# A fused attention and two-MoE kernel: batch 1 goes through the first MoE in two groups of tokens

## The chip, the cores and the metric

The kernel runs on one core of a Trainium2 chip. The metric is device time in microseconds of one execution, lower is better.

## The reference, cut to what matters

Four batches of 576 tokens, 8 heads of 64. Each row of scores keeps its 32 largest values; the attention output goes, token by token, through a dense "first MoE" (two products with 1536 columns, multiplied, and a product back to 512) and then through a second MoE in which each token goes to the one of 8 experts that its gate picks.

```python
scores = scale * np.matmul(q, k.transpose(0, 1, 3, 2))        # (4, 8, 576, 576)
kth = np.partition(scores, -top_k, axis=-1)[..., -top_k:-top_k + 1]
attn = softmax(np.where(scores >= kth, scores, -1e9))
x = (attn @ v) laid out as (2304, 512)
x = ((x @ w_a) * (x @ w_b)) @ w_out                            # first MoE, d_ff 1536
expert_idx = np.argmax(x @ w_gate, axis=1)                     # second MoE
out[mask] = gate_w[mask, None] * (np.maximum(x[mask] @ w1[e], 0) @ w2[e])
```

## The kernel before, in words

**Work and order.** The kernel is written as a list of operations with an engine, an estimated cost, a position and dependencies (class `Plan`). `Plan.emit` runs a list schedule over them once, when the program is built: at each step an engine takes the ready operation of the lowest position. What comes out is a fixed order for each engine; on the chip each engine runs its own list in that order and waits wherever an input is missing. SyncE issues the loads and stores, also in one fixed order.

**Attention.** The 576 tokens of a batch are two groups: g0 has 320 tokens, g1 has 256 (`GRP`). A head pair (p = 0 to 3) with a group is worked in tiles of 128 query rows: 5 tiles for g0, 4 for g1. A tile is: scores on TensorE (L601), copied by ScalarE (L606), the 32nd largest found on VectorE by MAX8 and MATCH_REPLACE8 (L625 to L652), the exponential on ScalarE (L633), masked on VectorE (L680), transposed on TensorE (L706). After the tiles of a group the product with v follows, which is called the *av* here: L727 and, last, L731. There are 8 av in a batch, 32 in all. Positions of attention are 10 times the tile's number, so attention goes ahead of everything else that is ready.

**Units.** Keys and queries of a head pair are loaded and prepared once for a *unit* (`load_unit`, `prep_unit`): k, q and v are loaded, k and q are split in a high and a low part (`hl`: ScalarE L512, GpSimd L514), transposed on TensorE (L523, 18 of 128x128), copied by ScalarE (L528, L531 and four small ones), and the transposed keys are copied once more by two DMAs (kS, L542). The buffers of raw k, raw q and `hl` exist once. The first 8 units (`FU`) take a shorter way in which k and q stay whole.

**First MoE.** `moe1(b, groups, xf, pos)` is called for the groups of a unit set when their attention is done. Its positions lie 1e5 higher than those of attention, so its matmuls fill what attention leaves of TensorE. It goes over 12 blocks of d_ff in two halves of 6. `ab` (L824) takes one weight block `wt` of 1 MiB (L802) and, for each group in `groups`, 24 matmuls; `l2` (L854) takes one block of 0.75 MiB (L842) and, for each group, 18 matmuls. A pass therefore loads 12 + 8 weight blocks, whatever the number of groups in it. `wt` has 3 buffers. A batch needs 288 L824 and 144 L854 matmuls with 320 columns (g0), and as many with 256 columns (g1). Then `gating(b, x2, groups, fill)` picks experts and scatters the rows.

**What sets the groups.** Batch 0 is in `HALVES`: its units are four for g0 and then four for g1, and `moe1` is called twice. The batches 1 to 3 have units that hold both groups, and `moe1` is called once, after the batch's last av:

```python
    for b in range(B):
        sets = [(g,) for g in (0, 1)] if b in HALVES else [(0, 1)]
        for groups in sets:
            for p in range(HP):
                for g in groups:
                    ...
                units.append((b, p, len(tiles), groups))
...
            if p == HP - 1 and g == groups[-1]:
                moe1(b, groups, XF[b], pos + 3)
```

After batch 3's attention the experts of the second MoE follow (L1136 to L1301), on rows that all batches have scattered. In the first 300 us the weights of the first MoE are also converted and stored (`conv`), and 8 fills of the scatter target are written (L345).

Of the kernel before, what the change touches and what calls it, by code (L numbers as in the profile page):

```python
# [209 lines left out]
def fused_kernel(ctx: ExitStack, tc: tile.TileContext, q, k, v, w_a, w_b, w_out, w_gate, w1, w2, out,  # L210
                 opts=None, dbg=None):
    nc = tc.nc
    opts = opts or {}
# [14 lines left out]
    OOB = 1.0e6  # L228
    HB = FB // 2
    CW = 512  # L230
    HALVES = opts.get("halves", (0,))
    FU = opts.get("fu", range(8))
    PE, ACT, DVE, POOL, SP = "PE", "ACT", "DVE", "POOL", "SP"

# [1074 lines left out]
# [3 lines that stand above are left out]
# [274 lines left out]
```

## Time and profile before

| | |
|---|---|
| median of 3 runs (range) | 1232.25 us (1228.04 to 1233.31) |
| the profiled execution's own time | 1233.15 us |
| its span in the trace | 1231.4 us |
| mean granted TensorE clock | 0.956 of 2.4 GHz |
| TensorE busy | 1103.6 us, 90% |
| VectorE busy | 896.3 us, 73% |
| ScalarE, GpSimd busy | 718.1 us, 460.6 us |
| DMA | 215.49 MB, mean 175 GB/s |

PE is TensorE, PEld its weight loads, DVE VectorE, ACT ScalarE, POOL GpSimd, SP SyncE. A row of busy time by stretch gives the stretch (us from the span's start), its length, then for PE, PEld, DVE, ACT and POOL (those that take part) busy us and the number of instructions, then the granted clock, the busy share of the DMA engines, and GB/s. A row of the timeline gives start, duration, engine, line, operation, tile written <- tiles read, shapes and count; in brackets the idle time just before, and what ended it. A row of costs gives the count, busy us and mean ns of one, then the idle time before. A row of DMA issues ends with KB of each and the median us from issue to landing; "q" behind an engine is its queue. L12 is line 12 of the kernel.

### The profile page before, as it was taken

Reading aid. Unit: us, or ns where it says so; the run is one execution under the profiler, and the core shown is the slowest. Engines: PE = TensorE matmul, PEld = TensorE weight load, DVE = VectorE, ACT = ScalarE, POOL = GpSimd, SP = SyncE. Lnnn points to the kernel's source line nnn. Section 1 sums busy time; section 2 is a strip of 40 time slices with the busy share of each in tenths; the row PEclk is TensorE's granted clock in tenths of the full one; section 3 lists DMA queues with packets and bytes.
Section 4 is the critical chain, followed back from the end, with each engine's and each line's share of the span. In section 5 each row is a group of like instructions: output and inputs, shape, how many; then the busy total and the mean of one; then the engine's idle time right before and its main releaser. Section 6 shows DMA issues by size and latency. Waiting matters only on the chain.

```text
span 1231.4 us, 22514 instructions
## 1 busy us (share of the span) xinstructions
PE 1103.6 (90%) x7710; PEld 981.2 (80%) x7710; DVE 896.3 (73%) x2636; ACT 718.1 (58%) x1567; POOL 460.6 (37%) x622
## 2 busy tenths in 40 slices
PE   4656796979999789999999999999999999999996
PEld 2333474868888579889888998989999899999996
DVE  6999999999998999999998999910004545444441
ACT  6667676776667567666765766633224445544551
POOL 3455566755536234234535422455234100000001
PEclk9966798989999999999999999999899999999998
DMA  8487578999677234244243442246535655554450
GB/s 235 130 276 229 164 245 261 323 303 300 208 255 248 93 87 144 109 153 144 78 152 112 132 151 104 86 155 225 191 147 184 189 152 174 176 177 151 159 177 22
DMA packets 116863, 215.49 MB, mean 175 GB/s; under 512 B 28883, under 2 KB 77011, under 8 KB 109061
## 3 DMA queue, kind: packets, MB, share of 16 engines
q1 hardware_dynamic: 113525, 204.52, 52.4%
q0 software_dynamic: 3216, 9.46, 2.0%
q8 instruction: 63, 1.03, 0.4%
q14 instruction: 59, 0.48, 0.1%
HBM read 171.82 MB, written 35.25 MB: 168 GB/s over the span
## 4 chain that ended last, share of the span: by engine, by line
PE 55%; DVE 14%; DMA 11%; issue 8%; ACT 7%; POOL 4%; SPq 1%; POOLq 0%; ACTq 0%; DVEq 0%
PE ab L824 16%; PE ab L854 9%; PE ab L1182 5%; PE pv L727 5%; DVE am L680 3%; DVE m L638 3%; PE ms L1231 3%; PE pv L1231 3%; PE sp L601 3%; DVE kt L641 2%; PE tp L706 2%; DMA xsort<-rows,pi 2%; DMA rawk<-in_k_dram 2%; DMA wt<-wos 1%; PE pv L731 1%
## 5 line engine op out<-in xcount | busy, mean ns | idle before, releaser
L824 PE MATMUL ab<-xh,wt 128*128 128x320 f32 (+1 forms) x1344 | 303.9, 304 | 3.9 <-ACT sb L809 3.8
L824 PEld LDWEIGHTS ab<-xh,wt 128*128 128x128 f32 x1344 | 227.6, 191 | 13.2 <-issue 7.8
L824 PE MATMUL ab<-xl,wt 128*128 128x320 f32 (+1 forms) x672 | 199.9, 297 | 0.0
L638 DVE MATCH_REPLACE8 m<-kt,m 128x288 f32<-128x288 f32 x432 | 188.5, 440 | 0.0
L641 DVE MAX8 kt<-m 128x8 f32<-128x288 f32 x432 | 182.3, 444 | 0.5
L854 PE MATMUL ab<-gH,wt 128*128 128x320 f32 (+1 forms) x768 | 171.8, 305 | 4.5 <-DMA wt<-wos 4.5
L680 DVE SCALAR_TENSOR_TENSOR am<-s,kt,e 128x576 f32<-128x576 f32 x144 | 139.8, 996 | 0.3
L854 PEld LDWEIGHTS ab<-gH,wt 128*128 128x128 f32 x768 | 130.7, 193 | 6.7 <-DMA wt<-wos 3.9
L832 POOL TENSOR_TENSOR sa<-sa,sb 128x320 f32<-128x320 f32 (+1 forms) x96 | 79.6, 829 | 145.0 <-ACT sb L809 144.5
L824 PEld LDWEIGHTS ab<-xl,wt 128*128 128x128 f32 x672 | 128.8, 192 | 0.0
L633 ACT ACTIVATE e<-s,nm 128x576 f32<-128x576 f32 x144 | 108.6, 778 | 11.6 <-POOL nm L628 11.3
L854 PE MATMUL ab<-gT,wt 128*128 128x320 f32 (+1 forms) x384 | 115.1, 300 | 0.0
L1256 POOL DMA_INDIRECT out_dram<-y,ti x23 | 23.0, 999 | 227.6 <-ACT y L1250 212.6
L1100 DVE TENSOR_TENSOR wp<-raw,wp 128x1024 fp32r<-128x1024 f32 (+1 forms) x73 | 67.4, 942 | 55.6 <-ACT wp L1099 55.2
L606 ACT COPY s<-sp 128x576 f32<-128x576 f32 x128 | 81.9, 640 | 42.9 <-PE sp L601 23.7
L706 PE MATMUL tp<-idr,am 128*128 128x128 f32 x512 | 84.8, 304 | 20.3 <-ACT aT L710 7.2
L401 POOL TENSOR_TENSOR gT<-sa,gH 128x320 fp32r<-128x320 f32 (+1 forms) x96 | 84.6, 881 | 45.8 <-ACT gH L400 45.4
L706 PEld LDWEIGHTS tp<-idr,am 128*128 128x128 f32 x512 | 64.1, 155 | 38.6 <-ACT aT L710 15.8
L1182 PE MATMUL ab<-xgh,wp 128*128 128x304 f32 (+6 forms) x352 | 89.4, 312 | 1.1 <-DVE gT L1189 0.7
L710 ACT COPY aT<-tp 128x512 f32<-128x512 f32 x128 | 72.4, 587 | 26.6 <-PE tp L706 25.8
L727 PE MATMUL pv<-aT,vt 128*64 128x320 f32 (+1 forms) x512 | 79.2, 451 | 6.5 <-ACT aT L695 4.5
L809 ACT ACTIVATE sa<-ab 128x320 f32<-128x320 f32 (+1 forms) x120 | 49.4, 412 | 53.9 <-PE ab L824 30.7
(303 smaller groups left out, 2560.8 us busy)
## 6 DMA issues: line engine op xcount, KB each, us to landing
wt<-ws SPq DMA_DIRECT2D x54, 1024.0 KB, 5.6
wt<-wos SPq DMA_DIRECT2D x44, 768.0 KB, 5.7
raw<-in_moe_w_dram SPq DMA_DIRECT2D x64, 512.0 KB, 3.7
kS<-kT SPq DMA_DIRECT2D x24, 304.0 KB, 4.5
xsort<-rows SPq DMA_DIRECT2D x8, 771.0 KB, 14.4
wp<-ws SPq DMA_DIRECT2D x6, 1024.0 KB
vt<-in_v_dram SPq DMA_DIRECT2D x20, 256.0 KB, 3.1
gT<-in_moe_w_a_dram SPq DMA_DIRECT2D x8, 512.0 KB, 4.1
```

The lines of the kernel that those rows point to most:

```text
L401: P(POOL, c_pool(cost), pos, lambda: nc.gpsimd.tensor_sub(lo(), src(), fr(hi())), r=rd + wh, w=wl)
L606: P(ACT, c_act(S), pos, lambda hf=hf, sp=sp: nc.scalar.copy(s()[:, :, hf * HS:(hf + 1) * HS], sp()[:, :, 0:HS]), r=[sp], w=[(s, (h, hf)) f ...
L633: P(ACT, c_act(S, True) + 90, pos, lambda h=h, e=e: nc.scalar.activation(e(), s()[:, h], AF.Exp, bias=nm()[:, h], scale=SCALE), r=[(s, (h, ...
L638: P(DVE, c_dve(HS), pos + 5.0 * h, lambda x=x, h=h, j=j: nc.vector.match_replace(out=m()[:, h], in_to_replace=kt(j, 8 * x - 8, 8 * x), in_ ...
L641: P(DVE, c_dve(HS), pos + 5.0 * h, lambda x=x, h=h, j=j: nc.vector.max(out=kt(j, 8 * x, 8 * x + 8), in_=m()[:, h]), r=[(m, h)], w=[KT(j, x)])
L680: P(DVE, c_dve(S) + 60, pos, lambda: nc.vector.scalar_tensor_tensor(am(), sc(), kth(), e(), op0=OP.is_ge, op1=OP.mult, accum_out=r.sum()[: ...
L706: res = nc.tensor.transpose(tp()[:, 512 * h + x * 128:512 * h + (x + 1) * 128], z()[:, 640 * h + x * 128:640 * h + (x + 1) * 128], idf)
L727: nc.tensor.matmul(pv()[64 * h:64 * h + 64, 0:n], u.vt()[:, h, j, :], r.aT[h]()[:, j, 0:n], start=(j == 0), stop=False)
L824: res = nc.tensor.matmul(pa()[:, 0:n], view()[:, m, wi, ko, :], xv()[:, ko], start=(ko == 0 and x == 0), stop=(ko == KO - 1 and x == 2))
L832: P(POOL, c_pool(n), pos, lambda: nc.gpsimd.tensor_mul(sa()[:, 0:n], sa()[:, 0:n], sb()[:, 0:n]), r=[sb], w=[sa])
L854: res = nc.tensor.matmul(pa()[:, 0:n], wv()[:, wi, f, :], gv()[:, f, :], start=(f == 0 and x == 0), stop=(f == HB - 1 and x == 2))
L1182: res = nc.tensor.matmul(pa()[:, 0:cap], p1[ko]()[:, wi, f * 128:(f + 1) * 128], xv()[:, ko], start=(ko == 0 and i == 0), stop=(ko == KO - ...
```

## The change

Batch 1 joins batch 0 in `HALVES`.

```diff
@@ -228,7 +228,7 @@
     OOB = 1.0e6
     HB = FB // 2
     CW = 512
-    HALVES = opts.get("halves", (0,))
+    HALVES = opts.get("halves", (0, 1))
     FU = opts.get("fu", range(8))
```

Batch 1 then has 8 units in place of 4: g0 of the four head pairs, then g1 of them. Its tiles are the same 36 in another order. `moe1` and `gating` are called for g0 after batch 1's fourth av and for g1 after its eighth. `FU` stays at 8 units, so batch 1's units all go the long way of `prep_unit`.

Since the schedule is made anew, the fixed orders shift from the 9th av on. The first place is TensorE just before the 16th av, which ends batch 1's attention; `tp` and `pv` are PSUM tiles, `am` the masked exponentials, `xh` and `xl` the parts of the first MoE's input, `hl` the split keys or queries. Before:

```order
L706 MATMUL tp<-idr,am 128x128 x8
L715 MATMUL pv<-idr,am 128x128
L601 MATMUL sp<-kT,qT 128x288
L601 MATMUL sp<-kS,qT 128x288
L601 MATMUL sp<-kT,qT 128x288
L601 MATMUL sp<-kS,qT 128x288
L523 MATMUL tp<-idr,hl 128x128 x4
L727 MATMUL pv<-aT_4907,vt 64x256
```

The same place now:

```order
L706 MATMUL tp<-idr,am 128x128 x4
L715 MATMUL pv<-idr,am 128x128
L824 MATMUL ab<-xh_2929,wt 128x320
L824 MATMUL ab<-xl_2942,wt 128x320
L824 MATMUL ab<-xh_2929,wt 128x320 x2
L824 MATMUL ab<-xl_2942,wt 128x320
L824 MATMUL ab<-xh_2929,wt 128x320
L523 MATMUL tp<-idr,hl 128x128 x4
L727 MATMUL pv<-aT_5312,vt 64x256
```

Matmuls of batch 1's g0 now stand between its last attention tiles. Between the 8th and the 16th av 660 matmuls of L824 and L854 stood before; now there are 762.

The second place is SyncE after the last fill of the scatter target, where units of batch 1 are loaded. `wt` are weight blocks of the first MoE, `rawk`, `rawq`, `vt`, `kS` belong to a unit. Before:

```order
L542 DMA kS<-kT 64x1216 x2
L842 DMA wt<-wos 128x1536
L802 DMA wt<-ws 128x2048
L440 DMA rawk<-in_k_dram 128x2x256
L440 DMA rawk<-in_k_dram 64x64
L802 DMA wt<-ws 128x2048
L440 DMA rawk<-in_k_dram 64x64
L440 DMA rawq<-in_q_dram 128x2x256
L440 DMA rawq<-in_q_dram 64x64 x2
L802 DMA wt<-ws 128x2048 x4
L842 DMA wt<-wos 128x1536
L440 DMA vt<-in_v_dram 128x2x256
```

The same place now:

```order
L542 DMA kS<-kT 64x1216 x2
L802 DMA wt<-ws 128x2048
L440 DMA rawk<-in_k_dram 128x2x256
L802 DMA wt<-ws 128x2048
L440 DMA rawk<-in_k_dram 64x64 x2
L440 DMA rawq<-in_q_dram 128x2x256
L440 DMA rawq<-in_q_dram 64x64 x2
L802 DMA wt<-ws 128x2048 x3
L842 DMA wt<-wos 128x1536
L440 DMA vt<-in_v_dram 128x2x256
```

Between a unit's keys (kS) and the next unit's first load (vt) eight weight blocks stood before, and six stand there now, since a unit of batch 1 is now one group long. Over the program there are 66 loads of L802 into `wt` in place of 54, 52 of L842 in place of 44, and four more units' loads.

The third place is TensorE at the 32nd and last av; `gH` and `gT` are the parts of the first MoE's inner result, all of batch 2 here. Before:

```order
L731 MATMUL pv<-aTt,vt 64x256 x2
L854 MATMUL ab<-gH_8125,wt 128x256
L854 MATMUL ab<-gT_8138,wt 128x256
L854 MATMUL ab<-gH_8125,wt 128x256 x2
L854 MATMUL ab<-gT_8138,wt 128x256
L854 MATMUL ab<-gH_8125,wt 128x256 x2
L854 MATMUL ab<-gT_8138,wt 128x256
L854 MATMUL ab<-gH_8125,wt 128x256 x2
```

The same place now:

```order
L731 MATMUL pv<-aTt,vt 64x256 x2
L854 MATMUL ab<-gH_8318,wt 128x256
L854 MATMUL ab<-gT_8330,wt 128x256
L854 MATMUL ab<-gH_8318,wt 128x256 x2
L854 MATMUL ab<-gT_8330,wt 128x256
L854 MATMUL ab<-gH_8318,wt 128x256
L854 MATMUL ab<-gH_8088,wt 128x320
L854 MATMUL ab<-gT_8113,wt 128x320
```

Before, 126 matmuls of batch 2 (54 with 320 columns, 72 with 256) stand between the last av and the first gating matmul of batch 2; now 42 do (18 and 24). From that gating matmul on TensorE's order is the same to the end.

## Rows read from the trace of the kernel before

**Rows 1.** The page: busy time, share of the span and instructions of each engine.
```profile
PE 1103.6 (90%) x7710; PEld 981.2 (80%) x7710; DVE 896.3 (73%) x2636; ACT 718.1 (58%) x1567; POOL 460.6 (37%) x622
```
**Rows 2.** Busy time by stretch, all engines, from batch 1's start to the end.
```profile
235.00:335.00 100.00, 89.21 (x649) 79.15 (x647) 95.40 (x307) 69.93 (x159) 54.98 (x71) 0.97 0.87 278
335.00:395.00 60.00, 57.01 (x465) 51.78 (x462) 57.41 (x186) 42.82 (x104) 28.75 (x41) 1.00 0.71 235
395.00:460.00 65.00, 53.21 (x365) 44.02 (x366) 60.57 (x196) 40.13 (x91) 20.61 (x34) 0.92 0.34 111
460.00:807.00 347.00, 339.30 (x2595) 308.70 (x2593) 320.03 (x1029) 228.83 (x529) 138.57 (x203) 1.00 0.38 124
807.00:1232.00 425.00, 404.94 (x2826) 389.40 (x2824) 143.69 (x292) 173.80 (x350) 85.97 (x116) 0.98 0.50 163
```
**Rows 3.** Busy time by stretch of lines L824 and L854 alone, after the last av.
```profile
807.80:1232.00 424.20, 83.92 (x576) 79.95 (x576) 0.98 0.50 163
...
807.80:1232.00 424.20, 58.30 (x414) 56.75 (x414) 0.98 0.50 163
```
**Rows 4.** Timeline of TensorE: the last av, and the pace of matmuls behind it.
```profile
807.14 0.65 PE L731 MATMUL pv<-aTt,vt 64*64 64x256 f32 x4
...
808.06 0.40 PE L854 MATMUL ab<-gH,wt 128*128 128x256 f32 x2
...
808.42 0.40 PE L854 MATMUL ab<-gH,wt 128*128 128x256 f32 x2
...
811.37 0.46 PE L854 MATMUL ab<-gH,wt 128*128 128x320 f32 x2
...
811.81 0.46 PE L854 MATMUL ab<-gH,wt 128*128 128x320 f32 x2
```
**Rows 5.** Busy time by stretch, in steps of 10 us, late in batch 1.
```profile
416.00:426.00 10.00, 6.12 (x41) 5.64 (x41) 10.00 (x32) 4.47 (x9) 3.59 (x7) 0.97 0.14 54
426.00:436.00 10.00, 8.81 (x50) 6.12 (x48) 10.00 (x37) 6.44 (x15) 2.00 (x5) 0.68 0.12 29
```
**Rows 6.** A unit's preparation: timeline of TensorE, then costs on ACT and POOL.
```profile
224.72 0.54 PE L523 MATMUL tp<-idr,hl 128*128 128x128 f32 x5
225.10 0.38 PE L854 MATMUL ab<-gH,wt 128*128 128x320 f32 x1
...
L512 ACT CAST hl<-rawk 128x576 fp32r<-128x576 f32 x12 | 8.1, 676 | 4.5 <-DMA rawk<-in_k_dram 4.5
...
L531 ACT CAST kT<-tp 128x512 fp32r<-128x512 f32 x24 | 14.1, 589 | 2.7 <-PE tp L523 2.4
...
L514 POOL TENSOR_TENSOR hl<-rawk,hl 128x576 fp32r<-128x576 f32 x12 | 17.8, 1483 | 14.3 <-ACT hl L512 14.2
```
**Rows 7.** Costs of gating on VectorE: the longest and shortest of its 12 operations.
```profile
L967 DVE TENSOR_TENSOR gb<-gb 128x24 f32<-128x24 f32 (+2 forms) x6 | 1.9, 312 | 0.1
...
L1005 DVE TENSOR_TENSOR cntb<-ms,cntb 128x8 f32<-128x8 f32 x6 | 1.0, 160 | 0.1
```
**Rows 8.** Chain of waits and timelines: a late weight block in batch 0's g1 pass.
```profile
388.61 6.26 DMA wt<-wos
...
395.01 0.36 PE L854 MATMUL ab<-gH,wt 128*128 128x256 f32 x1 [1.38 <-DMA wt<-wos]
...
401.47 0.76 DVE L614 TENSOR_TENSOR m<-sp,s 128x576 f32<-128x576 f32 x1 [3.39 <-ACT s L606]
```
**Rows 9.** DMA issues in 235 to 335 and 335 to 460; then 10 us by stretch.
```profile
wt<-ws SPq DMA_DIRECT2D x9, 1024.0 KB, 9.6
...
wt<-ws SPq DMA_DIRECT2D x10, 1024.0 KB, 5.6
...
286.00:296.00 10.00, 10.00 (x81) 8.71 (x80) 10.00 (x30) 7.20 (x17) 6.17 (x8) 1.00 1.05 318
```
**Rows 10.** Chain of waits: preparation of the unit after batch 1's end.
```profile
438.68 2.97 DMA rawk<-in_k_dram
...
442.53 1.75 POOL hl L514
```

## Prediction

> **What bounds the kernel now.** I read the page's engine table first, then busy time by stretch, then TensorE's timeline where a stretch looked odd, and last the chain of waits. TensorE is busy 90% of the span, VectorE 73% [rows 1], but these are averages over stages with different limits [rows 2]. From 235 to 460 us, batch 1's attention, VectorE is busy 95 to 96% and sets the pace; TensorE has holes: 10.8 us in the first 100, 3.0 in the next 60, and 11.8 in the last 65. In those last 65 us batch 0's first MoE has run out and batch 1's may not start, because its one call waits for the batch's last av; the clock falls with it, 0.92 on the mean, 0.68 in the worst 10 us [rows 5]. From 460 to 807 us TensorE is busy 98% and VectorE 92%: both are near their limit, and matmuls pile up. After the last av, which ends at 807.8 us [rows 4], VectorE has little to do and TensorE sets the end, 424 us long.
>
> What lies behind the last av is the point. 576 L824 and 414 L854 matmuls run there [rows 3]. Batch 3 by itself has 576 and 288, so 126 L854 matmuls are batch 2's, left over: a debt that goes back to the hole at 395 to 460.
>
> **The change part by part.**
>
> *Term 1, behind the last av: minus 11.1 us.* The new order leaves 42 matmuls of batch 2 there, 84 fewer: 36 with 320 columns, 48 with 256. Their pace there is three in 0.44 us (811.37 to 811.81) and three in 0.36 us (808.06 to 808.42) [rows 4], so 0.147 and 0.120 us each, and 36 x 0.147 + 48 x 0.120 = 5.3 + 5.8 = 11.1 us. All of it lies on the path, since TensorE does nothing else there and its order behind is the same. The cover shrinks from 16.6 us of matmuls to 5.5 (18 x 0.147 + 24 x 0.120); batch 3's g0 matmuls, whose input is ready by then, cover what comes after, so I cost the shorter cover at nothing. If they did not, the price would be a few tenths of a microsecond.
>
> *Term 2, TensorE up to the last av: plus 0.2 us.* Added: the same 84 matmuls, 11.1 us; four more unit preparations of 18 transposes, five of which take 0.38 us (224.72 to 225.10) [rows 6], so 72 x 0.076 = 5.5 us; a second set of gating matmuls, some 0.6 us by the same pace. That is 17.2 us. Recovered: between the 8th and the 16th av 762 matmuls stand where 660 stood, among the tiles where nothing stood before. If the stretch from 395 to 460 becomes like its neighbour behind, its 11.8 us of idle time go, and 8% of 65 us of slow clock, 5.2 us [rows 2]: 17.0 us. Both ends: if the 3.0 us before it go too, minus 2.8; if nothing could be filled, plus 17.2.
>
> *Term 3, VectorE up to the last av: nothing on the path, at most 2.3 us.* The second gating adds 12 operations of 160 to 312 ns, 2.3 us in sum [rows 7]. They fall after 433 us, where VectorE has 27 us of idle time [rows 2]. Without that cover they cost 2.3.
>
> *Term 4, ScalarE and GpSimd: nothing.* A unit's preparation costs ScalarE two splits of 0.68, four copies of 0.59 and about 1 us of small ones, 4.7 us, and GpSimd two of 1.48 [rows 6]: 18.9 and 11.9 us for four units, among 225 us in which they are idle about 72 and 121 us [rows 2]. If the cover fails, a unit starts late: see the third rival.
>
> *Term 5, weight blocks: plus 3.4 us.* Batch 1 loads 20 blocks more, 12 of 1 MiB and 8 of 0.75, 18 MiB; four units add 1.4 MiB each by their shapes (k, q and v of 288 KiB, two copies kS of 304 KiB). On average there is room, as the DMA engines are busy 71%, 34% and 38% from 335 us on [rows 2]. But a block in a pass of one group feeds 18 matmuls of 0.120 us, 2.2 us, or 24, at most 3.5 us, while a block takes 5.6 us to land, and 9.6 us when the DMA engines are crowded [rows 9]; with three buffers it arrives in time only if attention stands in between. The trace has one case where it did not, in batch 0's g1 pass: a block landed 6.26 us after its issue, TensorE waited 1.38 us, and VectorE, waiting for scores behind that, 3.39 us [rows 8]. Batch 0's two passes loaded 40 blocks; batch 1's two passes load as many, so I take one more such wait. Ends: 0 if every block is early, and for the other end the fourth rival.
>
> *Term 6, the crowded start: nothing taken, at most 7 us.* By the 11th av the new order wants three blocks and one unit more than before, 4.4 MiB; at the 318 GB/s of the most crowded 10 us [rows 9] that is 14.5 us of transfer, in a stretch of 100 us whose DMA share is 0.87 [rows 2]. The 13 us of room would nearly do. If they do not, I price it at half the transfer, 7 us. The Trainium skill, "Perfetto Trace Analysis", section "Identifying the Most-Contended Engine", says to judge DMA by bytes against the memory's peak, not by the engines' occupancy; by its 358 GB/s the 278 GB/s here leave 22% free and the bound would be 0. The rows speak against the page: landing went from 5.6 to 9.6 us at that rate.
>
> *Sum.* 1233.15 us (the profiled execution, 0.9 above the median shown) - 11.1 + 0.2 + 3.4 = 1225.7, so **about 1225 us** against the median of 1232.25, or 0.6% faster. A measurement of this kernel can tell about 0.5%, 6.2 us, from no change: faster means below 1226.1, slower above 1238.4.
>
> **The rivals.**
>
> *Second case, attention ends earlier.* From 460 to 807 us TensorE may be the slower of the two: only 7.7 us idle. Between the 16th and the last av the new order has 786 - 720 = 66 fewer matmuls with 320 columns and 48 more with 256, 9.7 - 5.8 = 3.9 us less, and the rest of the hole (3 us) goes. If TensorE alone paces there, the last av comes 7 us earlier: 1225.7 - 7 = 1219, or 1215 without the weight wait. [...]
>
> *Third case, units come late: no difference.* A unit of batch 1 is now 4 or 5 tiles long in place of 9, and raw k, raw q and the split exist once. At the next boundary after batch 1 the chain of waits does run through it: 2.97 us for raw k, 1.75 us for the split [rows 10], though VectorE was not idle. Four more boundaries of 2 us each, 8 us, or the 7 us of term 6, would give 1232 to 1234.
>
> *Fourth case, slower: weight blocks decide.* If the passes of batch 1 meet late blocks not once but six times (15% of 40 blocks), each costs VectorE 3.4 us as at 395 us, and batch 2's attention starts 20 us later: 1233.15 - 10.9 + 20.4 = 1243. The point is (6.2 + 10.9) / 3.4, five waits. For it: 3.5 us of work against a landing of 5.6. Against it: batch 0's 40 blocks, in a far more crowded stretch, met one.
>
> That the change does not do what it says is excluded by the new order.
>
> **How the numbers follow.** My forecast, with its own range of 1219 to 1229, has 0.45; the second case 0.14; the third, with term 6, 0.27; the fourth 0.14. The forecast lies at the edge of the 0.5%: I put 0.38 of its 0.45 below 1226.1. So faster is 0.38 + 0.14 = 0.52. The remaining 0.07 and the 0.27 of the third case make 0.34 within 0.5%. Slower is 0.14. The range for 8 in 10 reaches from 1214, the second case with 1 us to spare, to 1240, which takes in the third case and the beginning of the fourth.
>
> **What would show it.** Right: 576 and 330 matmuls of L824 and L854 behind the last av; that av within 5 us of 807; in batch 1's last 65 us TensorE busy over 95% at full clock. Term 5 is wrong if waits for `wt` in front of L824 or L854 are none, or several. The forecast falls if the last av comes more than 9 us later than 807: then the hole was filled and VectorE paid for it. The third case shows as idle time in front of L523 or L601 at each boundary of batch 1's units; the fourth as TensorE idle in front of L824 and L854, ended by a DMA into `wt`.

## The result: slower by 0.8%, and the profile after

| | before | after |
|---|---|---|
| median of 7 runs each, measured together | 1232.32 us | 1243.12 us (1241.43 to 1247.2) |
| ratio, 95% interval | | 1.0082 (1.006 to 1.0105) |
| profiled execution, its span | 1233.15, 1231.4 us | 1242.58, 1240.9 us |
| 16th av (end of batch 1's attention) | 433.1 us | 460.9 us |
| from the 16th to the 32nd av | 374.3 us | 374.2 us |
| from the 32nd av to the end | 424.0 us | 405.8 us |

The last three rows are the starts of an av's last L731 matmul, counted in the trace; they add up to the span. Such a column comes from one profile of each kernel; runs 4, 15 and 16 below, which leave batch 1 as it was, have their 16th av at 428.3 to 439.9 us, so a difference there of less than some 12 us decides nothing by itself. The forecast was 1225 us, so it was wrong by 18 us and by its sign. The loss has one place: 27.8 us more up to the 16th av. Behind the last av 18.2 us are won, more than was forecast.

The page's engine line answers to [rows 1]: every engine is busy a little longer.

```profile
PE 1111.5 (90%) x7790; PEld 987.8 (80%) x7790; DVE 900.4 (73%) x2648; ACT 733.9 (59%) x1608; POOL 475.8 (38%) x629
```

Seen from TensorE, the 9.5 us that the span grew are 7.9 us more of busy time and 1.6 more of idle time (span less busy: 127.8 us before, 129.4 now). The idle time that the change was to take away is all still there.

Busy time by stretch, cut at the same times as [rows 2]:

```profile
235.00:335.00 100.00, 79.03 (x546) 69.55 (x543) 78.84 (x237) 63.12 (x146) 49.22 (x55) 0.88 0.87 269
335.00:395.00 60.00, 56.30 (x448) 50.35 (x446) 49.74 (x165) 39.99 (x100) 28.42 (x46) 0.97 0.74 248
395.00:460.00 65.00, 62.83 (x500) 57.25 (x500) 61.88 (x199) 50.33 (x118) 39.13 (x50) 1.00 0.77 249
460.00:807.00 347.00, 334.23 (x2555) 302.74 (x2552) 327.22 (x1066) 230.40 (x529) 133.75 (x194) 1.00 0.50 170
807.00:1232.00 425.00, 417.49 (x2948) 398.85 (x2947) 164.65 (x359) 187.03 (x386) 92.02 (x125) 1.00 0.49 164
```

Read the busy times of TensorE and VectorE, the first and the third behind the comma. The hole at 395 to 460 was filled as forecast: TensorE 62.8 us busy of 65 in place of 53.2, at full clock. But VectorE, which sets the pace of batch 1's attention, fell from 95.4 to 78.8 us in the first 100, and from 57.4 to 49.7 in the next 60. From 235 to 460 us it is idle 34.5 us (225 less the three), where before it was idle 11.6.

So the same stretch, from the 8th to the 16th av, as one row for each kernel. Before:

```profile
235.30:433.10 197.80, 176.12 (x1313) 155.35 (x1311) 187.03 (x603) 134.61 (x311) 95.02 (x131) 0.97 0.72 235
```

After:

```profile
236.90:460.90 224.00, 197.16 (x1479) 176.49 (x1477) 189.47 (x593) 153.68 (x361) 116.08 (x147) 0.94 0.81 257
```

The stretch is 26.2 us longer: VectorE works 2.4 us more and waits 23.8 us more. Its waits from 235 to 465 us (waiting tile and line, what it waited for: total us, times, longest), before:

```profile
DVE m L614 <- ACT s L606: 5.7, 5, 3.4
...
DVE m L614 <- PE sp L601: 0.7, 1, 0.7
```

After, and then the two longest:

```profile
DVE m L614 <- PE sp L601: 15.9, 3, 11.5
DVE m L614 <- ACT s L606: 10.4, 5, 4.6
```

```profile
270.78 0.76 DVE L614 TENSOR_TENSOR m<-sp,s 128x576 f32<-128x576 f32 x1 [4.63 <-ACT s L606]
308.49 0.76 DVE L614 TENSOR_TENSOR m<-sp,s 128x576 f32<-128x576 f32 x1 [11.52 <-PE sp L601]
```

L614 is the first operation of a tile of 128 rows on VectorE: it wants scores. What the scores at 308 us waited for stands in the chain of waits (start, us, what; SPq is SyncE's queue) and, for the order of the loads, in SyncE's timeline:

```profile
290.67 0.83 SPq L542
...
292.23 0.54 SPq L440
...
293.52 12.13 DMA rawk<-in_k_dram
...
305.75 0.67 ACT hl L512
...
308.49 0.77 DVE m L614
```

```profile
281.42 3.20 SPq L345 DMA_DIRECT2D xsort<-rows  x3
284.73 5.84 SPq L842 DMA_DIRECT2D wt<-wos  x3
290.67 1.47 SPq L542 DMA_DIRECT2D kS<-kT  x2
292.23 2.09 SPq L440 DMA_DIRECT2D rawk<-in_k_dram  x3
```

A unit's raw k is asked for when the unit before it is prepared, since raw k exists once. Here it stood behind three fills, three weight blocks and the kS copies of the unit before. It comes in three loads, of 256, 16 and 16 KB; the first was issued at 292.23, the last at 293.52, and raw k was there 12.13 us after the last. TensorE's timeline shows what else came late:

```profile
285.99 0.75 PE L523 MATMUL tp<-idr,hl 128*128 128x128 f32 x4 [3.11 <-POOL hl L514]
291.43 0.75 PE L523 MATMUL tp<-idr,hl 128*128 128x128 f32 x4 [3.10 <-POOL hl L514]
295.30 0.63 PE L854 MATMUL ab<-gH,wt 128*128 128x320 f32 x1 [3.12 <-DMA wt<-wos]
304.75 0.37 PE L601 MATMUL sp<-kS,qT 128*128 128x288 f32 x1 [1.17 <-DMA kS<-kT]
```

Transposes waited twice for the split of `hl`, a weight block of batch 0 arrived at 295.3 us, and kS, asked for at 290.67, at 304.75. Then the copy of these scores (L606) stood in ScalarE's fixed order behind the split of the next unit's raw k (L512), whose wait ended at 305.75:

```profile
305.75 0.67 ACT L512 CAST hl<-rawk 128x576 fp32r<-128x576 f32 x1 [1.68 <-DMA rawk<-in_k_dram]
306.33 0.58 ACT L710 COPY aT<-tp 128x512 f32<-128x512 f32 x1
306.81 0.65 ACT L606 COPY s<-sp 128x576 f32<-128x576 f32 x1
```

The chain of waits names only what came last. kS alone held these scores to 304.75, and their matmuls ended at 305.4. Waiting for raw k put off their copy from there to 306.81, so raw k cost an estimated 1.4 us of the 11.5; the split, the weight block and kS, one behind the other in TensorE's order, fit most of the rest.

In steps of 10 us: VectorE works 0.59 us from 296 to 306, with a DMA share of 1.00; the granted clock is 0.50 of 2.4 GHz, the lower of its two levels, in the 10 us after TensorE had been busy under 4 of 10:

```profile
276.00:286.00 10.00, 3.96 (x26) 3.20 (x24) 10.00 (x33) 4.23 (x9) 9.39 (x11) 0.80 0.77 224
286.00:296.00 10.00, 3.06 (x15) 2.51 (x16) 9.72 (x28) 4.61 (x9) 3.29 (x5) 0.50 1.00 318
296.00:306.00 10.00, 7.74 (x49) 7.23 (x48) 0.59 (x3) 4.11 (x12) 1.12 (x2) 0.85 1.00 256
```

Behind the last av the counts are the forecast ones, 576 and 330, in answer to [rows 3]:

```profile
835.50:1241.00 405.50, 81.89 (x576) 77.64 (x576) 0.99 0.50 166
...
835.50:1241.00 405.50, 45.79 (x330) 44.28 (x330) 0.99 0.50 166
```

L854 is down by 12.5 us and L824 by 2.0. Another 4 us came with a stall of before that had not been in the sum, and that has no counterpart now:

```profile
864.06 0.58 PE L824 MATMUL ab<-xh,wt 128*128 128x256 f32 x1 [3.77 <-ACT sb L809]
```

### The profile page after: what moved, and what is told of

Its sections match the earlier page's. It is cut to its first block, busy times and chain, and to the rows that moved or that the text cites. A ratio compares the mean times of both kernels' runs of the same rounds, so it can differ in the third digit from the quotient of the medians.

```text
span 1240.9 us, 22843 instructions
## 1 busy us (share of the span) xinstructions
PE 1111.5 (90%) x7790; PEld 987.8 (80%) x7790; DVE 900.4 (73%) x2648; ACT 733.9 (59%) x1608; POOL 475.8 (38%) x629
## 4 chain that ended last, share of the span: by engine, by line
PE 51%; DMA 7%; DVE 7%; issue 6%; ACT 3%; POOL 2%; SPq 1%; POOLq 0%; ACTq 0%; DVEq 0%
PE ab L824 14%; PE ab L854 9%; PE ab L1182 6%; PE pv L727 3%; PE ms L1231 3%; PE pv L1231 3%; PE sp L601 3%; DMA wt<-wos 3%; PE tp L706 2%; DMA rawk<-in_k_dram 2%; DVE m L638 1%; DVE am L680 1%; PE tp L523 1%; DVE kt L641 1%; PE pv L731 1%
## 5 line engine op out<-in xcount | busy, mean ns | idle before, releaser
L824 PE MATMUL ab<-xh,wt 128*128 128x320 f32 (+1 forms) x1344 | 304.1, 305 | 1.9 <-ACT sb L809 1.7
L824 PEld LDWEIGHTS ab<-xh,wt 128*128 128x128 f32 x1344 | 227.5, 191 | 8.9 <-issue 5.9
L824 PE MATMUL ab<-xl,wt 128*128 128x320 f32 (+1 forms) x672 | 200.3, 298 | 0.2 <-POOL xl L794 0.2
L854 PE MATMUL ab<-gH,wt 128*128 128x320 f32 (+1 forms) x768 | 172.4, 304 | 12.1 <-DMA wt<-wos 12.0
L854 PEld LDWEIGHTS ab<-gH,wt 128*128 128x128 f32 x768 | 130.2, 192 | 16.3 <-DMA wt<-wos 10.8
L832 POOL TENSOR_TENSOR sa<-sa,sb 128x320 f32<-128x320 f32 (+1 forms) x96 | 82.1, 855 | 132.7 <-ACT sb L809 127.6
L824 PEld LDWEIGHTS ab<-xl,wt 128*128 128x128 f32 x672 | 128.9, 192 | 0.5 <-POOL xl L794 0.5
L854 PE MATMUL ab<-gT,wt 128*128 128x320 f32 (+1 forms) x384 | 114.4, 298 | 0.0
L606 ACT COPY s<-sp 128x576 f32<-128x576 f32 x128 | 82.2, 642 | 38.9 <-PE sp L601 23.4
L706 PE MATMUL tp<-idr,am 128*128 128x128 f32 x512 | 79.7, 297 | 15.2 <-ACT qT L503 4.4
L727 PE MATMUL pv<-aT,vt 128*64 128x320 f32 (+1 forms) x512 | 80.6, 457 | 6.7 <-ACT aT L695 4.3
L614 DVE TENSOR_TENSOR m<-sp,s 128x576 f32<-128x576 f32 x64 | 47.7, 746 | 39.7 <-PE sp L601 22.1
```

The lines of the kernel that those rows point to most:

```text
L606: P(ACT, c_act(S), pos, lambda hf=hf, sp=sp: nc.scalar.copy(s()[:, :, hf * HS:(hf + 1) * HS], sp()[:, :, 0:HS]), r=[sp], w=[(s, (h, hf)) f ...
L706: res = nc.tensor.transpose(tp()[:, 512 * h + x * 128:512 * h + (x + 1) * 128], z()[:, 640 * h + x * 128:640 * h + (x + 1) * 128], idf)
L727: nc.tensor.matmul(pv()[64 * h:64 * h + 64, 0:n], u.vt()[:, h, j, :], r.aT[h]()[:, j, 0:n], start=(j == 0), stop=False)
L824: res = nc.tensor.matmul(pa()[:, 0:n], view()[:, m, wi, ko, :], xv()[:, ko], start=(ko == 0 and x == 0), stop=(ko == KO - 1 and x == 2))
L832: P(POOL, c_pool(n), pos, lambda: nc.gpsimd.tensor_mul(sa()[:, 0:n], sa()[:, 0:n], sb()[:, 0:n]), r=[sb], w=[sa])
L854: res = nc.tensor.matmul(pa()[:, 0:n], wv()[:, wi, f, :], gv()[:, f, :], start=(f == 0 and x == 0), stop=(f == HB - 1 and x == 2))
```

## The experiments

Theories, with the letters that the recorded expectations use. A: units of batch 1 are late because their loads stand in the DMA crowd of 235 to 312 us. B: the doubled weight blocks (the fourth case). C: a unit of 4 or 5 tiles is prepared too slowly wherever it is. D: the chain of a unit (load, split, transposes, kS copy) is longer than its tiles; E: it is the added work on the engines. D1 and D2: the long way of preparation is dear only in the crowd, or for every split unit. F, G and H are told in the texts themselves.

All runs at a glance. Ratios are to the kernel before in the same measurement; the last three columns are counted as in the table above.

| run | median us | ratio, 95% interval | 16th av | 16th to 32nd | behind |
|---|---|---|---|---|---|
| 1 units split, one call | 1261.51 | 1.0227 (1.019 to 1.0264) | 463.8 | 376.4 | 416.8 |
| 2 units whole, two calls | 1227.1 | 0.9954 (0.9935 to 0.9972) | 433.1 | 373.6 | 415.6 |
| 3 change, fills early | 1236.27 | 1.003 (1.0014 to 1.0047) | 444.4 | 380.4 | 407.3 |
| 4 batch 2 split, not 1 | 1248.09 | 1.0113 (1.0083 to 1.0143) | 439.9 | 384.0 | 420.2 |
| 5 change, loads ahead | 1248.62 | 1.0123 (1.0093 to 1.0153) | 453.5 | 378.9 | 413.6 |
| 6 change, short way | 1231.28 | 0.9971 (0.9953 to 0.9989) | 427.6 | 382.1 | 420.5 |
| 7 before, loads ahead | 1227.03 | 0.9944 (0.9926 to 0.9963) | 424.0 | 376.8 | 423.7 |
| 8 whole, two calls, batches 1 and 2 | 1231.44 | 0.9978 (0.9957 to 0.9998) | 431.0 | 377.8 | 419.1 |
| 9 change, short way for g0 | 1226.05 | 0.9944 (0.9909 to 0.9979) | 441.7 | 373.9 | 408.4 |
| 10 change, loads ahead, fills early | 1228.69 | 0.9977 (0.9958 to 0.9996) | 439.6 | 383.1 | 403.8 |
| 11 whole, two calls, loads ahead | 1225.68 | 0.9941 (0.9917 to 0.9964) | 424.5 | 379.0 | 421.0 |
| 12 run 11, fills early | 1225.32 | 0.993 (0.9902 to 0.9958) | 436.5 | 371.7 | 415.4 |
| 13 before, short way batch 1 | 1228.27 | 0.9957 (0.9936 to 0.9978) | 428.6 | 373.5 | 426.7 |
| 14 run 1, short way | 1229.46 | 0.9973 (0.9957 to 0.9988) | 428.3 | 383.0 | 416.5 |
| 15 run 4, short way batch 2 | 1241.49 | 1.0081 (1.0055 to 1.0107) | 434.4 | 385.7 | 419.6 |
| 16 before, short way batch 2 | 1223.61 | 0.9924 (0.9896 to 0.9952) | 428.3 | 370.8 | 420.5 |
| 17 run 2, short way batch 2 | 1230.81 | 0.9981 (0.996 to 1.0002) | 428.3 | 380.0 | 420.0 |
| 18 run 2, short way batches 1, 2 | 1219.57 | 0.989 (0.9868 to 0.9912) | 425.0 | 373.6 | 419.5 |

### The two halves of the change, apart

Run 1 splits the units but calls the first MoE once; run 2 leaves the units whole and calls it for each group.

```diff
 run 1, on the changed kernel
-                moe1(b, groups, XF[b], pos + 3)
+                if b != 1:
+                    moe1(b, groups, XF[b], pos + 3)
+                elif groups == (1,):
+                    moe1(b, (0, 1), XF[b], pos + 3)
 run 2, on the kernel before
-            if p == HP - 1 and g == groups[-1]:
+            if p == HP - 1 and b == 1:
+                moe1(b, (g,), XF[b], pos + 3)
+            elif p == HP - 1 and g == groups[-1]:
```

> Batch 1's units are split by group as in the change, but its first MoE is one call for both groups after its last av, so the weight blocks are loaded once. Theory A (late unit loads in the DMA crowd of 235 to 312 us): the VectorE waits of that stretch stay and nothing is gained, 1240 to 1252 us. Theory B (20 more weight blocks come late): back to 1228 to 1236. Theory C (short units are prepared too slowly wherever they stand): as A, 1240 to 1252, with waits at every boundary of batch 1's units.

> Batch 1's units hold both groups as before, but its first MoE is called once for g0 and once for g1, so the weight blocks are loaded twice. Theory A: 1228 to 1236, no difference from before. Theory B: slower than before, 1240 or more, with 5 or more waits for wt on TensorE. Theory C: 1228 to 1236.

Run 1, with no weight block more than before, is 28 us slower, and shows the same wait at the same place:

```profile
306.34 0.76 DVE L614 TENSOR_TENSOR m<-sp,s 128x576 f32<-128x576 f32 x1 [11.19 <-PE sp L601]
```

The late block of batch 0 stands ahead of it here too, so that is no block of the second call:

```profile
293.43 0.63 PE L854 MATMUL ab<-gH,wt 128*128 128x320 f32 x1 [3.81 <-DMA wt<-wos]
```

That run 1 loses more than the change fits TensorE's idle time: it may not begin batch 1's first MoE before the batch's end, and is idle 38.6 us from the 8th to the 16th av (21.7 before, 26.8 in the changed kernel).

Run 2, with all of the doubled blocks, is 0.5% faster. Its waits for them up to the last av come to 3.7 us on TensorE:

```profile
PE ab L854 <- DMA wt<-wos: 1.9, 1, 1.9
PE ab L824 <- DMA wt<-ws: 1.8, 2, 1.3
```

B falls: the loss is the split units', and with whole units the second call is a gain. It lies behind the last av (415.6 us in place of 424.0), as the prediction meant it. The two halves do not add up: 2.3% lost and 0.5% won would be 1.8%, and the change lost 0.8%, so the second call is worth more where units are late.

### The crowd, and a batch without one

Run 3 issues seven of the 8 fills at 69 to 120 us, where all of them stood at 229 to 285; run 4 splits batch 2, where no fills and no conversion run.

```diff
 run 3, on the changed kernel (two places)
-opts.get("fo", 0)
+opts.get("fo", 1)
 run 4
-    HALVES = opts.get("halves", (0, 1))
+    HALVES = opts.get("halves", (0, 2))
```

> The change, with the 8 fills of the scatter target issued among tiles 8 to 15 of batch 0 and not in 217 to 284 us. Theory A: the longest waits of VectorE before 312 us go, the last av comes 10 to 20 us earlier than 835, 1222 to 1234 us. Theories B and C: 1240 to 1246, since the weight blocks and the unit boundaries are the same.

> Batch 2 in place of batch 1 goes in two groups, where the DMA engines are busy under 40% and TensorE has no hole. Theory A: 1229 to 1236, neither gain nor loss. Theory B: 36 MiB of weights in batch 2 cost what they cost in batch 1, 1238 or more. Theory C: eight short units cost the same there, 1240 or more.

Without the fills in the crowd the 16th av comes 16.5 us earlier than in the changed kernel, and the median is 6.9 us lower, so a large part of the delay there is the crowd's. But a batch outside the crowd loses as much time, 1.1%, and A alone doesn't explain that. The chain of waits of run 4 does run through a unit's DMAs:

```profile
470.49 5.75 DMA rawk<-in_k_dram
...
549.33 8.42 DMA kS<-kT
...
592.90 7.28 DMA kS<-kT
```

Run 4's order is that of before nearly up to the 16th av, and still its profile is 6.8 us later there: that much is the spread of a column.

### The chain of a unit: loads ahead, and the short way

Run 5 gives raw k and raw q a second buffer and lets a unit's loads go one unit ahead; run 6 prepares batch 1's split units by the short way, in which k and q stay whole and no kS is copied; run 7 is run 5's edit with whole units.

```diff
 runs 5 and 7
-opts.get("raw", 1)
+opts.get("raw", 2)
-load_unit(ui + 1, b2, p2, g2, pos - 60, U[ui].mark)
+load_unit(ui + 1, b2, p2, g2, pos - 60, U[max(ui - 1, 0)].mark)
 run 6
-    FU = opts.get("fu", range(8))
+    FU = opts.get("fu", range(16))
```

> The change, with two buffers for raw k and raw q in place of one, and a unit's loads held back by the preparation of the unit two before and not of the one before. All work and its engines stay. Theory D (the chain of a unit, from its load's issue over split and transposes to the kS copy, does not fit into 4 or 5 tiles): the landing of raw k, 5 to 12 us, leaves the chain, VectorE's longest wait before 312 us falls under 4 us, 1222 to 1236 us. Theory E (the added work of four preparations on TensorE, ScalarE and GpSimd slows attention): 1240 to 1246.

> The change, with all 16 units of batches 0 and 1 on the short way of preparation: no split of k and q and no kS copies, but scores on TensorE from whole numbers, which take longer. Theory D: the boundaries' waits go, the last av comes earlier than 835 although TensorE has some 10 us more of scores, 1228 to 1240 us. Theory E: ScalarE and GpSimd lose 25 us of work but TensorE, which is the full engine, gets more: 1245 or more.

> The kernel before with the same two buffers and earlier loads: the control. Theory D: a unit of 9 tiles leaves room for the chain, so 1228 to 1236, no difference. Theory E: the same. If it gains as much as the change does, the loads were late in both and the test says nothing of the split.

Run 5 missed. A wait of the same length was there, 10 us earlier, and not for raw k:

```profile
298.69 0.76 DVE L614 TENSOR_TENSOR m<-sp,s 128x576 f32<-128x576 f32 x1 [10.79 <-ACT s L606]
```

In TensorE's order the next unit's scores now stood behind an av (its L727 took 741 ns in the median, at a granted clock of 0.58 from 286 to 296 us), and VectorE waited for both. The 16th av came 7 us earlier only, which is within the spread, and the new order left 90 matmuls of batch 2 behind the last av in place of 42, so that the end is 7.8 us longer. Run 6 has no split of k and no kS, and there the long wait is gone; the 16th av comes 33 us earlier than in the changed kernel:

```profile
296.55 0.76 DVE L614 TENSOR_TENSOR m<-sp,s 128x576 f32<-128x576 f32 x1 [2.23 <-ACT s L606]
```

Not all of that reaches the end: the last av comes 25 us earlier than in the changed kernel, and behind it 14.7 us are given back (420.5 against 405.8).

### Two calls in batch 2 too

```diff
 run 8, on the kernel before
+            if p == HP - 1 and b in (1, 2):
+                moe1(b, (g,), XF[b], pos + 3)
```

> The kernel before with whole units, and the first MoE of batches 1 and 2 called once for each group (weights loaded twice in both). Theory D: no harm from 36 MiB more, the debt behind the last av falls as in the run that did it for batch 1, 1222 to 1231 us. If double weight blocks do cost something, it shows twice here: 1232 or more.

By the ratios, which are each to before in the same measurement, run 8 has half of run 2's gain (0.2 in place of 0.5%), and the two intervals overlap: a second doubled pass shows no gain of its own.

### Crowd or every unit, and what the cures add up to

Run 9 uses the short way for the four units of batch 1's g0 alone (`range(12)`), those that stand in the crowd. Run 10 is run 5 with the fills early, run 11 is run 2 with loads ahead, run 12 is run 11 with the fills early.

> The change, with only the first four units of batch 1 (its g0, which fall into the DMA crowd) on the short way, the other four on the long way. Theory D1 (the long way is dear only where its loads and kS copies stand behind the fills and weight blocks of the crowd): the 12th av near 352 us in place of 374, the 16th near 437, 1222 to 1234 us. Theory D2 (every one of the eight long units costs alike): half of the loss stays, 1236 to 1241.

> The change with loads one unit ahead and the fills issued early, both. Theory D1: with neither the loads nor the fills in the way, the 16th av comes at 430 to 440 us, and the total is 1225 to 1236. Theory D2: no better than the early fills alone, 1236 or more.

> No split of units: the kernel before with loads one unit ahead and batch 1's first MoE in two calls, each of which alone gave about 1227. If they act in different places (the units' chain before the last av, the debt behind it), 1220 to 1225; if both do the same thing, 1226 to 1230.

> As the run before it in this list, and the fills early too. Theory D1: fewer bytes in the crowd help the loads and weight blocks there, 1217 to 1225. Theory D2: no difference from that run.

Run 9 takes back the whole loss, 17 us, with g1's units still split and by the long way; run 10 takes back 14 with all of them by the long way. Run 10 has as many instructions on every engine as the changed kernel, and nearly the same busy times:

```profile
PE 1105.8 (90%) x7790; PEld 986.1 (80%) x7790; DVE 900.7 (73%) x2648; ACT 731.5 (60%) x1608; POOL 476.0 (39%) x629
```

So the added work (E) is not what makes the loss; it hangs on when loads and fills are issued. Run 12 is run 10 with whole units, in the same measurement: there splitting costs 3.4 us (1228.7 against 1225.3), where without the two edits it costs 16 (1243.1 against run 2's 1227.1). Loads ahead without the fills do not do it: run 5 is 23 us above run 11. In batch 1, then, it is mostly the long way in the crowd that is dear (D1). The 16th av of both is 6 to 9 us later than before, which is within the spread. Runs 11 and 12 are not told apart from run 2, or from each other.

### The controls: whole or split, long or short

In runs 6 and 9 the short way could have saved time for whole units as well. Runs 13 and 16 give it to whole units, runs 14 and 15 to split ones.

```diff
 run 13, on the kernel before
+    FU = opts.get("fu", range(12))
 run 14, on run 1
+    FU = opts.get("fu", range(16))
 run 15, on run 4
+    FU = opts.get("fu", tuple(range(8)) + tuple(range(12, 20)))
 run 16, on the kernel before
+    FU = opts.get("fu", tuple(range(8)) + tuple(range(12, 16)))
```

> The kernel before (units whole) with the short way for batch 1's four units too. It is the control for the run in which all split units went the short way: 1231.3 us beside 1243.1 for the change, 11.8 us less, 33 us less at the 16th av. Theory F (it is split and long way together that is dear: a unit of 4 or 5 tiles is too short for the chain load, split, transposes, kS): with whole units the chain is covered, so little changes, the 16th av at 428 to 436 us, 1226 to 1235 us. Theory G (the short way saves this much wherever it stands, split or not): the 16th av 20 us or more earlier, 413 us or less, and about 1221 us.

> The run with batch 1's units split and one call of the first MoE (1261.5 us, 16th av at 463.8 us), now with the short way for all 8 units of batch 1. F: the 16th av returns to 425 to 440 us, and the time to 1228 to 1240 us. Rival E (splitting a batch adds work to the engines and disorders the tiles, however a unit is prepared): the 16th av stays at 450 us or later, and the time at 1248 us or more. One call in place of two is dearer than the run with two calls and the short way by about 4 us in any case (batch 1's first MoE starts late).

> The run with batch 2 split in place of batch 1 (1248.1 us; from the 16th to the 24th av 190 us, 185 before), now with the short way for batch 2's 8 units, batch 1 whole and by the long way. F: a unit's chain is on the path in batch 2 too, with no crowd; with the short way the 16th to the 24th av takes 178 to 186 us and the time falls to 1224 to 1236 us. Rival H (there the dearness is TensorE's, which has no hole for more work and a batch whose matmuls come in another order): 188 us or more stay, and 1242 us or more.

> The control for the run before it: the kernel before with the short way for batch 2's four whole units. F: no great change, 1226 to 1237 us, the 16th to the 24th av 180 to 187 us. G: 12 us or more less than before, about 1221 us. If the short way is dearer for TensorE, which is near its limit there, slower than before by a few us.

For batch 1 the four corners (median us, 16th av):

| batch 1's units | long way | short way |
|---|---|---|
| whole | 1232.3, 433.1 | 1228.3, 428.6 (run 13) |
| split, two calls | 1243.1, 460.9 | 1231.3, 427.6 (run 6) |
| split, one call | 1261.5, 463.8 | 1229.5, 428.3 (run 14) |

The short way is worth some 4 us to whole units and 12 to 32 to split ones. Splitting delays the 16th av by 28 to 31 us by the long way and by nothing (1.0 and 0.3 us less) by the short one. F holds in batch 1: it is the split and the long way together. Runs 6 and 14 alone would not decide against E, since the short way also takes work off ScalarE and GpSimd (713.8 and 447.6 us busy in run 6, 733.9 and 475.8 in the changed kernel); run 10 does. Even so, by the short way splitting gains nothing over whole units (1231.3 and 1229.5 us beside 1228.3), and what was expected of run 14 missed in one point: one call is no dearer than two there, so the second call, too, is worth something only in some of the corners.

Batch 2 is another matter. In run 15 the 16th to the 24th av took 185.2 us, as F said; but the time stayed at 1241.5 us, as H said, and the loss shows only by the 32nd av. The whole stretch from the 16th to the 32nd av, before (columns as in [rows 2]):

```profile
433.10:807.40 374.30, 362.70 (x2757) 328.31 (x2755) 346.08 (x1111) 246.87 (x572) 148.26 (x216) 1.00 0.38 121
```

Run 4:

```profile
439.90:823.90 384.00, 372.67 (x2846) 336.73 (x2844) 351.36 (x1130) 261.60 (x609) 164.26 (x232) 1.00 0.55 177
```

Run 15:

```profile
434.40:820.10 385.70, 375.19 (x2767) 322.87 (x2763) 346.61 (x1124) 243.51 (x563) 142.59 (x219) 1.00 0.50 162
```

TensorE is busy 10.0 and 12.5 us longer than before, and the stretch takes 9.7 and 11.4 us more; idle it is 11.3 and 10.5 us, as before (11.6). In run 4 the costs by line show 72 more transposes of L523 there than before, 194 in place of 122, and 8.6 us more busy in them:

```profile
L523 PE MATMUL tp<-idr,hl 128*128 128x128 f32 x194 | 23.2, 247 | 2.9 <-POOL hl L514 2.9
```

This fits H: from 433 us on TensorE is near its limit, and work added to it becomes time. It is an agreement of two numbers in two runs; no run took that work out alone, and run 16 shows that it is no rule:

```profile
428.30:799.10 370.80, 366.88 (x2720) 314.66 (x2718) 346.64 (x1116) 240.10 (x550) 142.47 (x209) 1.00 0.36 117
```

There TensorE is busy 4.2 us longer than before and the stretch is 3.5 us shorter, because TensorE's idle time fell to 3.9 us. In time run 16 lies between F and G: 1223.6 us.

### A version that beats both

> Whole units, batch 1's first MoE called once for each group, and the short way for batch 2's units: the two single edits that gave most (1227.1 and 1223.6 us, 5 and 9 us below before). If their gains are of different stretches and add up: about 1219 us. If both draw on the same thing (matmuls of the first MoE that come earlier, attention that is held up less): 1222 to 1225 us.

> The same with batch 1's units by the short way too (1228.3 us alone, 4 us below before). If a whole unit's long way costs something in every batch: 2 to 4 us less than the run before it, about 1216 us. If TensorE has no room for the two calls in batch 1 once attention goes faster: no less than it.

Run 18 keeps the units whole, calls batch 1's first MoE for each group and prepares batches 1 and 2 by the short way: 1.1% faster than before, and the fastest of all. Run 17, which leaves batch 1 by the long way, missed by some 6 us: 380.0 us from the 16th to the 32nd av, where run 16 with the same units took 370.8. Why is open. Gains of single edits don't add up here; each edit makes a new order, which may be why.

## Why the prediction was wrong, by its own steps

- **The opening reading**, VectorE busy 95 to 96% from 235 to 460 us, holds for the first 160 us; in the last 65 it is 93% (60.57 of 65) [rows 2].
- **Term 1** held: 84 matmuls fewer, and L854 12.5 us shorter where 11.1 were priced. The end won 18.2 us, since L824 took 2.0 us less and the stall of 3.77 us went too; neither was in the sum.
- **Term 2** held where it was priced: the hole was filled. Its sum, plus 0.2, did not: up to the last av TensorE is busy 22.6 us longer and idle 5.1 us longer, since a hole opened at 276 to 306 us instead, which is the third case's.
- **Term 3** held: the 12 added operations stand behind the 16th av, where gating has 30 operations in place of 18 and takes 1.8 us more (2.3 were priced), in a stretch that is no longer than before. The 2.4 us that VectorE works more in batch 1 are not these, near as the number is: gating has 30 operations there in both kernels.
- **Term 4 is the step that failed:** "ScalarE and GpSimd: nothing. [...] If the cover fails, a unit starts late". I compared busy times with idle times of two engines. What the runs showed in its place is 23.8 us more of waiting on VectorE from the 8th to the 16th av, gone with the short way (run 6: VectorE waits 12.0 us there, 10.8 before) and over half gone when the loads and fills of the same work are issued earlier (run 10: 21.3 us, against 34.5). The cost was the length of a chain over four places: raw k's landing, the split, the transposes, and kS's landing. A whole unit has 9 tiles to hide it, a split one 4 or 5, and the next load may not start before the chain ends. I had also not asked what is queued behind a waiting L512: the copies that attention lives on.
- **Term 6 failed in size:** "nothing taken, at most 7 us". Without the fills in the way (run 3) the 16th av is 16.5 us earlier. I had priced bytes against room on the DMA engines; what counted is when a load lands that is issued behind others: kS was waited for until 14 us after its issue at 290.67, and raw k's last 16 KB landed 12.13 us after theirs. The Trainium skill, "Perfetto Trace Analysis", section "Identifying the Most-Contended Engine", judges DMA by bytes against the memory's peak, which gave a bound of 0 here; the measurement at 256 to 318 GB/s and a DMA share of 1.00 speaks against it more than my 7 us did.
- **Term 5**, 3.4 us, was not what the doubled blocks cost. TensorE's waits for L854's blocks are now six, 8.2 us, up to the last av, where one stood. But three of them, 6.2 us, stand before 410 us and are for blocks of batch 0; run 1, without doubled blocks, has four there, 6.4 us. The other three, at 569 to 626 us, come to 2.0 us. The doubled blocks are no cause: run 1 loses more without them, and run 2 gains with them.

```profile
PE ab L854 <- DMA wt<-wos: 8.2, 6, 3.1
```

- **The rivals.** The third case named the right mechanism, "units come late", and the right sign in front of L523. It priced 8 us, from four boundaries of 2 us each as after batch 1's end [rows 10], where the DMA share is 0.12 to 0.34 [rows 2, 5]; in the crowd one boundary alone cost VectorE 11.5 us, and the 16th av came 27.8 us later. Since the point where gain and loss meet was some 18 us, that size decided the sign. The fourth case gave 1243 us, the measured time, and six late blocks, the number counted, but half of those are batch 0's and run 2 refutes the reason: a right number is no evidence for its mechanism.
- **The second case** did not come: 374.2 us from the 16th to the 32nd av, 374.3 before. Runs 4 and 15 fit TensorE setting the pace there, run 16 only in part. The same page and section of the Trainium skill would judge TensorE's room by weight-load time, 336.7 and 322.9 us in runs 4 and 15, by which 12 to 16% were free. In run 15 that time is 5.4 us lower than before and the stretch 11.4 us longer, so its length does not follow weight-load time; run 16 shows that it does not follow matmul time alone either.
- **The test I wrote** told it: "if the last av comes more than 9 us later than 807: then the hole was filled and VectorE paid for it." It came 27.7 us later. VectorE paid by waiting, though, not by work.

**What stays open:** how much of run 4's and run 15's loss is the added TensorE work and how much the order; why run 17 gives less than the single edits in it, and run 11 no more than either of its own; and why the second call helps whole units by the long way and not split ones by the short way.

## What to carry to other kernels

When a change cuts a stage into shorter pieces, compare the length of the preparation chain of one piece, with landings at the DMA share of that very stretch, with the length of the piece; idle time of the engines did not tell it here. Split a change into its halves before believing either: here one half (two calls) gained 0.5%, and the other lost 2.3%; and measure them together too, for they did not add up. Where TensorE is near its limit, count the preparation's matmuls too; that this is what batch 2 paid was argued here, not shown.

## What the runs showed of the hardware that was not expected

A small load that is issued behind large ones takes long: raw k's last 16 KB landed 12.13 us after their issue, behind fills, weight blocks and kS copies at a DMA share of 1.00, and 2.97 us after it in a quiet stretch [rows 10]. A whole block of 1 MiB took 9.6 us in the median from 235 to 335 us before [rows 9]. And a wait of attention slows TensorE too, once it idles: the granted clock fell to 0.50 from 286 to 296 us, after 10 us in which TensorE had been busy 3.96.
